# The sign of 64-bit weights through ScalarE's parametric ReLU, norms split in two steps, softmax denominators on VectorE

## The chip, the cores and the metric

The kernel runs on one core of a Trainium2 chip. The core has five engines that run their own instruction lists in order: TensorE (PE, with its weight loads as PEld), VectorE (DVE), ScalarE (ACT), GpSimd (POOL) and SyncE (SP), which issues all DMAs of this kernel. The metric is the device time of one execution in microseconds, as the median of several.

## The reference

Attention over 4 batches, 12 heads, 448 positions and 64 columns, with a cap on the scores, and behind it a two-layer network over the 1792 tokens:

```
scores = cap * tanh(q @ k.T / 8 / cap)
attn   = exp(scores) / (sum(exp(scores)) + 1e-9)      # rows of 448
x      = (attn @ v), heads joined                     # 1792 x 768
h      = x @ w_in                                     # 768 x 2048
g      = s * max(h, 0)**2 + b
out    = g @ w_out                                    # 2048 x 768
```

q, k and v are float32. The weights w_in and w_out come as float64: the kernel reads each as two 32-bit words and makes a float32 of them on the chip.

## The kernel before, in words

**Work.** Scores are taken for pairs of heads; a pair has three blocks of 128 keys (chunks), and two pairs share one block for the last 64 keys. A chunk goes PE (scores, line 512), ACT (tanh, line 516), ACT (exp, line 520). The product with v (line 570) and the row sums (line 578) follow in two runs for each pair, one over chunks 0 and 1, one over chunk 2 and the shared block; such a run is called a half-pair here, and there are 48 of them. ACT then copies the sums out of PSUM (line 598). `normal` sends the row sums through SBUF and DRAM and takes their reciprocals. Both layers run in 16 bit, each product as three matmuls (high by high, high by low, low by high).

**Weights.** `piece` loads a block of 128 x 512 doubles as pairs of words (line 654) and makes float32 of it in four operations: two on DVE for the low word and the sign (`sign`, lines 662 and 663), one multiplication by 2^-112 on DVE or POOL (lines 434, 436), and one on DVE that joins the words (`join`, line 666). `win` does that for three blocks of w_in, squares them (on ACT line 700, DVE 701 or POOL 702), sums the squares on PE (line 712), sends the largest through a second small matmul (`lanes`, line 477), and has a scale from both (`fin`). With it the block is split into two 16-bit parts (lines 433, 453). There are eight such groups of w_in. The first two lie in a tensor named gt until the first layer needs it, the others in tiles named w.

**Order.** The program is written by a planner: `Plan.emit` takes all operations with a rank, a duration that the author estimated and the engines that may do them, and places the one that can start first. So the order on every engine, and for some operations the engine, follow from the numbers in `CHOICE`. Each engine runs its list strictly in that order: an instruction that waits holds everything behind it on its engine. PSUM has two buffers for scores, so PE can be two chunks ahead of tanh.

Of the kernel before, what the change touches and what calls it, by code (L numbers as in the profile page):

```python
# [243 lines left out]
def arrange(units, at):  # L244

    key = {}
    for name, pre, _ in units:
# [5 lines left out]
    'bias': 1.806,  # L253
    'shy': {'DVE': 0.3, 'POOL': 0.5},
# [36 lines left out]
    'late': 0.621,  # L291
    'lag': 0.0,
    'cling': 19.274,
# [4 lines left out]
    'tail': 0.9,  # L298
    'evac': ('ACT',),
    'sq': ('ACT', 'DVE', 'POOL'),  # L300
    'expo': ('DVE', 'POOL'),
# [24 lines left out]
def attention_moe_kernel(  # L326
# [196 lines left out]
    def normal(bb, c2, rank):  # L523
# [15 lines left out]
        def whole():  # L539
            a = P[kc][:, 0]  # L540
            nc.gpsimd.tensor_tensor(a, a, P[kc][:, 1], ALU.add)
            nc.gpsimd.tensor_scalar(a, a, guard[:, 0:1], 0.0, ALU.add, ALU.add)

        gps(0.55, rank, whole, r=["guard", *((kc, h, i) for h in range(2) for i in range(2))], w=[kc], port=True)
        dve(0.32, rank, lambda: nc.vector.reciprocal(P[kc][:, 0], P[kc][:, 0]), w=[kc])
# [14 lines left out]
    def pv(bb, c2, rank, step):  # L560
# [54 lines left out]
        def gather():  # L615
# [6 lines left out]
            r=[("xm", bb, c) for c in range(NP)], w=[("xn", bb)], port=True,  # L622
# [24 lines left out]
    def piece(kr, src, n, rank, over=()):  # L647
# [13 lines left out]
        def sign():  # L661
            nc.vector.tensor_scalar(lo(), lo(), 29, None, ALU.logical_shift_right)
            nc.vector.scalar_tensor_tensor(lo(), hi(), -0x80000000, lo(), ALU.bitwise_and, ALU.bitwise_or)
# [22 lines left out]
    def win(g, rank):  # L686
# [36 lines left out]

        dve(0.38, rank, most, r=[kp], w=[("wnm", g)])
        kl = lanes(("wps", g), rank, g, [("wnm", g)])

        def fin():
            nc.vector.tensor_copy(n[:, 1:2], P[kl][:, 0:1])
            root2(n)
# [466 lines left out]
    m2s = []  # L1196
# [68 lines left out]
```

## Time and profile before

| | |
|---|---|
| median of 3 runs | 640.17 us (638.66 to 641.72) |
| the profiled execution | 639.61 us |
| its span, first to last instruction | 637.8 us |
| PE busy | 627.0 us, 98% of the span |
| DVE, ACT, POOL busy | 400.2, 351.7, 208.1 us |
| moved by DMA | 101.67 MB, 159 GB/s over the span |

The span is what lies between the first and the last instruction in the profile; the execution's own time is 1.8 us longer. Busy time counts the stretches in which at least one instruction of an engine runs. PE is close to always busy, so the views to read are those that show when it isn't: its waits, and the windows in which its busy time is under the window's length or its clock (PEclk, as a share of 2.4 GHz) is under 1. The first 90 us are nearly only attention and preparing of w_in; then the first layer's products fill PE.

### The profile page before, as it was taken

The page shows a single profiled execution, that of the slowest core. Times are in us where ns is not written, and L with a number is a line of the kernel's source. Part 1 is how long each engine was busy: PE and PEld are TensorE (multiplying, and loading weights), DVE is VectorE, ACT ScalarE, POOL GpSimd, SP SyncE. Part 2 cuts the span into 40 slices and gives each one's busy share as a digit, 9 for nine tenths or more (in the row PEclk, how much of TensorE's full clock was granted, in tenths as well). Part 3 has the DMA queues.
Part 4 walks back from the last instruction along what each step waited for, and adds up shares of the span by engine and source line. Part 5 has one row for each costly group of instructions (what it writes and reads, how often), then busy time and mean ns, then how long its engine had stood idle before and what let it go on. Part 6 is the DMA issues. An engine that isn't in the chain of part 4 may idle for free.

```text
span 637.8 us, 11435 instructions
## 1 busy us (share of the span) xinstructions
PE 627.0 (98%) x4404; PEld 331.4 (52%) x4404; DVE 400.2 (63%) x810; ACT 351.7 (55%) x472; POOL 208.1 (33%) x238
## 2 busy tenths in 40 slices
PE   7999899999999999999999999999999999999997
PEld 2332344344444433434454445555558996556997
DVE  5986857888797878788773341577767222537322
ACT  5889787886884585684674531346354002445100
POOL 3343511546456544466151020117643000105000
PEclk9999899999999999999999999999999999999999
DMA  8766423654262775853854013385412774001671
GB/s 301 293 184 193 124 86 107 215 175 143 60 234 59 251 211 179 272 200 92 282 195 157 1 48 128 146 280 212 164 48 89 239 260 147 1 2 53 223 256 67
DMA packets 54774, 101.67 MB, mean 159 GB/s; under 512 B 16192, under 2 KB 34752, under 8 KB 54720
## 3 DMA queue, kind: packets, MB, share of 16 engines
q1 hardware_dynamic: 54720, 100.95, 48.2%
q8 instruction: 34, 0.56, 0.4%
q14 instruction: 20, 0.16, 0.1%
HBM read 82.58 MB, written 18.17 MB: 158 GB/s over the span
## 4 chain that ended last, share of the span: by engine, by line
PE 85%; DMA 8%; DVE 3%; ACT 1%; SPq 1%; POOL 1%; issue 0%; ACTq 0%
PE ps_v L570 9%; PE ps_m L1003 9%; PE ps_s L512 7%; PE ps_s L1003 6%; PE ps_m L843 6%; PE ps_s L844 6%; PE ps_m L844 6%; PE ps_s L843 6%; PE ps_m L845 6%; PE ps_s L845 6%; PE ps_m L1094 5%; PE ps_m L1095 5%; PE ps_m L1096 5%; PE ps_v L578 4%; DMA gt<-in_w_in 2%; DMA w<-in_w_out 2%
## 5 line engine op out<-in xcount | busy, mean ns | idle before, releaser
L1003 PEld LDWEIGHTS <-w 128*128 128x128 f16 x1008 | 96.6, 98 | 1.0
L516 ACT ACTIVATE bed<-ps_s,arena 128x896 f32<-128x896 f32 x84 | 81.5, 1006 | 9.9 <-PE ps_s L512 8.2
L520 ACT ACTIVATE bed<-bed,par 128x896 f32<-128x896 f32 x84 | 84.2, 1040 | 0.2
L570 PE MATMUL ps_v<-bed 128*32 128x448 f32 x768 | 83.0, 548 | 0.8 <-ACT pw L598 0.6
L512 PE MATMUL ps_s<-bed 64*128 64x448 f32 (+1 forms) x384 | 80.6, 578 | 1.9 <-DMA bed<-in_qT 1.6
L1094 PE MATMUL ps_m<-gt,w 128*128 128x448 f16 x192 | 67.7, 353 | 0.0
L843 PE MATMUL ps_m<-x,w 128*128 128x448 f16 x192 | 67.7, 353 | 0.0
L1096 PE MATMUL ps_m<-gt,w 128*128 128x448 f16 x192 | 67.7, 353 | 0.0
L844 PE MATMUL ps_s<-x,w 128*128 128x448 f16 x192 | 67.7, 353 | 0.0
L844 PE MATMUL ps_m<-x,w 128*128 128x448 f16 x192 | 67.7, 353 | 0.0
L845 PE MATMUL ps_m<-x,w 128*128 128x448 f16 x192 | 67.7, 353 | 0.0
L843 PE MATMUL ps_s<-x,w 128*128 128x448 f16 x192 | 67.7, 353 | 0.0
L1095 PE MATMUL ps_m<-gt,w 128*128 128x448 f16 x192 | 67.7, 352 | 0.0
L845 PE MATMUL ps_s<-x,w 128*128 128x448 f16 x192 | 67.7, 352 | 0.0
L843 PEld LDWEIGHTS <-w 128*128 128x128 f16 x384 | 37.5, 98 | 37.3 <-issue 2.1
L845 PEld LDWEIGHTS <-w 128*128 128x128 f16 x384 | 37.5, 98 | 35.0
L844 PEld LDWEIGHTS <-w 128*128 128x128 f16 x384 | 37.6, 98 | 33.8
L512 PEld LDWEIGHTS ps_s<-bed 64*128 64x128 f32 (+1 forms) x384 | 27.4, 177 | 43.5 <-issue 12.2
L938 ACT ACTIVATE pw<-ps_s,arena 128x448 f32<-128x448 f32 x32 | 20.1, 632 | 52.6 <-PE ps_s L845 49.7
L570 PEld LDWEIGHTS ps_v<-bed 128*32 128x32 f32 x768 | 20.3, 109 | 51.4 <-issue 35.7
L444 POOL TENSOR_TENSOR pw<-pw 128x224 f32<-128x224 f32 x24 | 21.6, 912 | 77.6 <-ACT pw L942 71.2
L578 PE MATMUL ps_v<-bed,ones 128*32 128x448 f32 x288 | 45.5, 545 | 0.0
(142 smaller groups left out, 1012.8 us busy)
## 6 DMA issues: line engine op xcount, KB each, us to landing
w<-w SPq DMA_DIRECT2D x48, 512.0 KB, 4.9
w<-in_w_out SPq DMA_DIRECT2D x24, 512.0 KB, 5.0
w<-ws SPq DMA_DIRECT2D x24, 512.0 KB, 4.9
w<-in_w_in SPq DMA_DIRECT2D x18, 512.0 KB, 5.5
bed<-in_v SPq DMA_DIRECT2D x24, 256.0 KB, 4.2
ws<-w SPq DMA_DIRECT2D x12, 512.0 KB, 2.9
bed<-in_kT SPq DMA_DIRECT2D x24, 224.0 KB, 3.3
bed<-in_qT SPq DMA_DIRECT2D x24, 224.0 KB, 3.6
```

What stands on the lines that cost most here:

```text
L512: nc.tensor.matmul(P[kp][o, h, 0:S], keys, P[q][rows], start=True, stop=True)
L516: 1.01, rank, lambda: nc.scalar.activation(P[kh], P[kp][:, :, 0:S], AF.Tanh, scale=tsc[:, 0:1]),
L520: 1.04, rank, lambda: nc.scalar.activation(P[kh], P[kh], AF.Exp, scale=par[:, 0:1]), r=["par"], w=[kh],
L570: nc.tensor.matmul(P[kp][o, 0, 0:S], P[kv][:, c, o], prob(c, h), start=(c == 0), stop=(c == NC))
L578: nc.tensor.matmul(P[kp][o, 1, 0:S], w, ph, start=first, stop=last)
L843: nc.tensor.matmul(ps[:, 0:S], wh, x[:, 0], start=(c == 0), stop=False)
L844: nc.tensor.matmul(ps[:, 0:S], wh, x[:, 1], start=False, stop=False)
L845: nc.tensor.matmul(ps[:, 0:S], wl, x[:, 0], start=False, stop=(c == NP - 1))
L1003: nc.tensor.matmul(at(), w(g, zw), b(g, zb), start=g == 0 and x == 0, stop=g == n - 1 and x == 2,)
L1094: nc.tensor.matmul(ps[:, 0:S], wh, ghi[:, f], start=(f == 0), stop=False)
L1095: nc.tensor.matmul(ps[:, 0:S], wh, glo[:, f], start=False, stop=False)
L1096: nc.tensor.matmul(ps[:, 0:S], wl, ghi[:, f], start=False, stop=(f == NF - 1))
```

## The change

Four edits in the code, and a new set of numbers for the planner:

- `piece` takes three operations for four. The sign no longer gets an operation of its own. The high word, read as a float, is scaled by 2^-112 where it is positive and by 2^-80 where it is negative; the shift by three in `join` then moves the extra exponent bit into the sign. ACT does that in one instruction, a parametric ReLU with scale 2^-112 and slope 2^32 (Prelu), or DVE does it in two (a multiplication, and a minimum with itself times 2^32). POOL no longer takes part. The low word's shift (`low`) no longer stands ahead of the scaling.
- In `win` the part of `fin` that needs only the group's own norm becomes `own`, which does not wait for the second small matmul.
- The reciprocals of the row sums (`whole` in `normal`) go from two POOL instructions and one on DVE to two on DVE.
- Three planner flags (`port`) go, and two lists of prerequisites name all groups where they named one.
- The ranks, `late`, `lag`, `bias` and `cling` are new, so the order on all engines is new. `late` is the margin in us that the planner leaves ahead of the small matmuls on PE: 0.621 before, 0.274 now; `lag`, that of all other PE operations, goes from 0 to 0.176.

```
--- before.py
+++ after.py
@@ -250,55 +250,55 @@
-    'bias': 1.806,
+    'bias': 1.658,
...
-        ('a', 0, 0): (-88.4, 62.61), ('a', 0, 2): (80.2, 2.4), ('a', 0, 4): (227.3, 40.55),
...
+        ('a', 0, 0): (19.2, 53.25), ('a', 0, 2): (20.0, 0.01), ('a', 0, 4): (161.4, 23.63),
+        ('a', 1, 0): (22.0, 75.07), ('a', 1, 2): (1029.6, 0.0), ('a', 1, 4): (985.8, 0.01),
...
-    'late': 0.621,
-    'lag': 0.0,
-    'cling': 19.274,
+    'late': 0.274,
+    'lag': 0.176,
+    'cling': 17.125,
...
+    'expo': ('ACT', 'DVE'),
     'evac': ('ACT',),
     'sq': ('ACT', 'DVE', 'POOL'),
-    'expo': ('DVE', 'POOL'),
@@ -538,11 +538,12 @@
 
         def whole():
             a = P[kc][:, 0]
-            nc.gpsimd.tensor_tensor(a, a, P[kc][:, 1], ALU.add)
-            nc.gpsimd.tensor_scalar(a, a, guard[:, 0:1], 0.0, ALU.add, ALU.add)
-
-        gps(0.55, rank, whole, r=["guard", *((kc, h, i) for h in range(2) for i in range(2))], w=[kc], port=True)
-        dve(0.32, rank, lambda: nc.vector.reciprocal(P[kc][:, 0], P[kc][:, 0]), w=[kc])
+            nc.vector.scalar_tensor_tensor(a, a, guard[:, 0:1], P[kc][:, 1], ALU.add, ALU.add)
+            nc.vector.reciprocal(a, a)
+
+        dve(
+            0.38, rank, whole, r=["guard", *((kc, h, i) for h in range(2) for i in range(2))], w=[kc], port=True,
+        )
         z = zd[bb * NP + c2]
         dma(3584, rank, lambda: nc.sync.dma_start(z, P[kc][:, 0]), r=[kc], w=[("z", bb, c2)], move=0.2)
         kr = buf(("rd", bb, c2), "rd", [128, S], F32)
@@ -619,7 +620,7 @@
         dve(
             0.28, rank,
             gather,
-            r=[("xm", bb, c) for c in range(NP)], w=[("xn", bb)], port=True,
+            r=[("xm", bb, c) for c in range(NP)], w=[("xn", bb)],
         )
         kl = lanes(("xps", bb), rank, NG + ND + bb, [("xn", bb)])
 
@@ -658,16 +659,26 @@
         hi = lambda: P[kr][:, :, 1]
         hf = lambda: P[kr].bitcast(F32)[:, :, 1]
 
-        def sign():
+        def low():
             nc.vector.tensor_scalar(lo(), lo(), 29, None, ALU.logical_shift_right)
-            nc.vector.scalar_tensor_tensor(lo(), hi(), -0x80000000, lo(), ALU.bitwise_and, ALU.bitwise_or)
 
         def join():
             nc.vector.scalar_tensor_tensor(hi(), hi(), 3, lo(), ALU.logical_shift_left, ALU.bitwise_or)
 
-        dve(0.25 + n * 0.0018, rank, sign, r=[kr], w=[(kr, "s")], port=True)
-        scaled(CHOICE["expo"], n, rank, hf, hf, 2.0 ** -112, [(kr, "s")], [kr])
-        dve(0.07 + n * 0.0011, rank + 0.5, join, r=[kr, (kr, "s")], w=[(kr, "f")], port=True)
+        def two():
+            nc.vector.tensor_scalar(hf(), hf(), 2.0 ** -112, None, ALU.mult)
+            nc.vector.scalar_tensor_tensor(hf(), hf(), 2.0 ** 32, hf(), ALU.mult, ALU.min)
+
+        ways = {
+            "ACT": (
+                0.29 + n * 0.00084,
+                lambda: nc.scalar.activation(hf(), hf(), AF.Prelu, scale=2.0 ** -112, alpha=2.0 ** 32),
+            ),
+            "DVE": (0.36 + n * 0.00158, two),
+        }
+        P.any({e: ways[e] for e in engines(CHOICE["expo"])}, rank, [kr], [(kr, "h")], port=True)
+        dve(0.16 + n * 0.00052, rank, low, r=[kr], w=[(kr, "s")], port=True)
+        dve(0.07 + n * 0.0011, rank + 0.5, join, r=[kr, (kr, "s"), (kr, "h")], w=[(kr, "f")], port=True)
         return hf
 
     def raw_buf(key, n):
@@ -724,15 +735,21 @@
         dve(0.38, rank, most, r=[kp], w=[("wnm", g)])
         kl = lanes(("wps", g), rank, g, [("wnm", g)])
 
+        def own():
+            root2(n[:, 0:1])
+            nc.vector.reciprocal(ip[:, 0:1], n[:, 0:1])
+            nc.vector.tensor_scalar(wn[:, g:g + 1], n[:, 0:1], n[:, 0:1], None, ALU.mult)
+
+        dve(0.85, rank + 0.1, own, r=[("wnm", g)], w=[("wnm", g, 0)])
+
         def fin():
             nc.vector.tensor_copy(n[:, 1:2], P[kl][:, 0:1])
-            root2(n)
-            nc.vector.reciprocal(ip, n)
-            nc.vector.tensor_tensor(wn[:, g:g + 1], n[:, 0:1], n[:, 0:1], ALU.mult)
+            root2(n[:, 1:2])
+            nc.vector.reciprocal(ip[:, 1:2], n[:, 1:2])
             nc.vector.tensor_scalar(sw, ip[:, 1:2], 8192.0, None, ALU.mult)
             nc.vector.tensor_scalar(wc[:, g:g + 1], ip[:, 0:1], n[:, 1:2], 1.0 / 2097152.0, ALU.mult, ALU.mult)
 
-        dve(1.75, rank, fin, r=[kl], w=[("wnm", g), ("wc", g)], port=True)
+        dve(1.5, rank, fin, r=[kl, ("wnm", g, 0)], w=[("wnm", g), ("wc", g)])
         for c in range(NC3):
             hi = lambda c=c: w1[g][:, 0, c].rearrange("p a b -> p (a b)")
             lo = lambda c=c: w1[g][:, 1, c].rearrange("p a b -> p (a b)")
@@ -798,8 +815,7 @@
             nc.vector.tensor_copy(brief[:, NG + d:NG + d + 1], m1)
 
         dve(
-            0.68, rank, amax, r=[("wc", g) for g in range(NG)] + [("om", d, q) for q in range(NQ)], w=[("om", d)],
-            port=True,
+            0.68, rank, amax, r=[("wc", g) for g in range(NG)] + [("om", d, q) for q in range(NQ)], w=[("om", d)]
         )
         kl = lanes(("ops", d), rank, NG + d, [("om", d)])
 
@@ -807,7 +823,7 @@
             pow2(p, P[kl][:, 0:1], si, iswo[:, d:d + 1], 1e-30)
             nc.vector.tensor_scalar(sc, wn, si, None, ALU.mult)
 
-        dve(1.3, rank, fin, r=[kl], w=[("op", d), ("os", d)], port=True)
+        dve(1.3, rank, fin, r=[kl], w=[("op", d), ("os", d)])
         half = NQ // 2
         for q in range(NQ):
             part = lambda e, q=q: P[kw[q // half]][:, (q % half) * QF:(q % half + 1) * QF, e]
@@ -1190,7 +1206,7 @@
     for g in range(NG):
         put(("w", g), [], lambda rank, step, g=g: win(g, rank))
     for d in range(ND):
-        put(("o", d), [("w", NG - 1)], lambda rank, step, d=d: wout(d, rank))
+        put(("o", d), [("w", g) for g in range(NG)], lambda rank, step, d=d: wout(d, rank))
     for p in range(ND // 2):
         put(("p", p), [("o", 2 * p), ("o", 2 * p + 1)], lambda rank, step, p=p: mix(p, rank, step))
     m2s = []
@@ -1198,7 +1214,7 @@
         m1s, fast = [], j in CHOICE["fast"]
         for f in range(NG if fast else NF):
             g = f if fast else f // 2
-            pre = [("a", j, NP - 2), ("w", g), ("w", CHOICE["alias"] - 1), *m2s]
+            pre = [("a", j, NP - 2), ("w", g), *(("w", a) for a in range(CHOICE["alias"])), *m2s]
             one = m1pair if fast else m1
             put(("m1", j, f), pre, lambda rank, step, j=j, f=f, one=one: one(j, f, rank))
             m1s.append(("m1", j, f))
```

Both programs hold the same number of matmuls and of DMAs. On the other engines the counts change: 28 of the 48 blocks get ACT's Prelu, 20 the two DVE instructions; of 38 multiplications, 24 additions and 24 scalings that went from POOL none is left there. The order of the pairs changes too: batch 0 is no longer finished before batch 1 begins, and PE has 21 half-pairs before the first product of the first layer, where it had 17.

SP's list from its start, before. In it kT, qT and v are the attention's inputs for a pair, in_w_in a block of w_in, and par the three scalars.

```order
L1140 DMA par<-in_cap 128x1
L488 DMA bed<-in_kT 128x448
L490 DMA bed<-in_qT 128x448
L654 DMA w<-in_w_in 128x1024 x3
L488 DMA bed<-in_kT 128x448
L490 DMA bed<-in_qT 128x448
L1140 DMA par<-in_s 128x1
L1140 DMA par<-in_b 128x1
L494 DMA bed<-in_v 128x512 x2
L654 DMA gt<-in_w_in 128x1024
L488 DMA bed<-in_kT 128x448
```

The same place in the changed program:

```order
L655 DMA gt<-in_w_in 128x1024
L1156 DMA par<-in_cap 128x1
L488 DMA bed<-in_kT 128x448
L490 DMA bed<-in_qT 128x448
L1156 DMA par<-in_s 128x1
L1156 DMA par<-in_b 128x1
L488 DMA bed<-in_kT 128x448 x2
L655 DMA gt<-in_w_in 128x1024
L490 DMA bed<-in_qT 128x448 x2
L494 DMA bed<-in_v 128x512 x3
L655 DMA w<-in_w_in 128x1024 x3
L655 DMA gt<-in_w_in 128x1024 x2
```

One block of w_in (for gt) now stands ahead of the first pair's kT and qT, and the second pair's qT comes behind 2.2 MB where it came behind 2.5 MB. The third block for gt, the first of the two in the last row here, has 5.3 MB ahead of its end.

ACT's list from its start, before. Lines 516 and 520 are tanh and exp of a chunk, line 700 a square of a weight block, line 598 the copy of the sums out of PSUM.

```order
L1153 ACT_TABLE_LOAD
L1153 ACTIVATE arena<-par 128x1
L516 ACTIVATE bed<-ps_s,arena 128x896 x2
L520 ACTIVATE bed<-bed,par 128x896 x2
L516 ACTIVATE bed<-ps_s,arena 128x896 x2
L700 ACTIVATE bed<-w 128x512
L520 ACTIVATE bed<-bed,par 128x896 x2
L516 ACTIVATE bed<-ps_s,arena 128x896 x2
L520 ACTIVATE bed<-bed,par 128x896
L598 ACTIVATE pw<-ps_v 128x896
```

The same place in the changed program, where line 675 is Prelu, line 711 the square, line 599 the copy:

```order
L675 ACT_TABLE_LOAD
L675 ACTIVATE gt<-gt 128x512
L1169 ACTIVATE arena<-par 128x1
L711 ACTIVATE bed<-gt 128x512
L516 ACTIVATE bed<-ps_s,arena 128x896 x2
L520 ACTIVATE bed<-bed,par 128x896 x2
L516 ACTIVATE bed<-ps_s,arena 128x896 x2
L520 ACTIVATE bed<-bed,par 128x896 x2
L675 ACTIVATE w<-w 128x512
L675 ACTIVATE gt<-gt 128x512
L516 ACTIVATE bed<-ps_s,arena 128x896 x2
L520 ACTIVATE bed<-bed,par 128x896
```

Ahead of the first tanh there now stand a Prelu and a square of the first block for gt, and ahead of the fifth tanh the Prelus of a block in w and of the third block for gt.

## Rows read from the trace of the kernel before

**Rows 1.** The page's first part, busy time of each engine and its share
```profile
PE 627.0 (98%) x4404; PEld 331.4 (52%) x4404; DVE 400.2 (63%) x810; ACT 351.7 (55%) x472; POOL 208.1 (33%) x238
```

**Rows 2.** waits of PE: engine, tile, line <- releaser: us in total, times, longest
```profile
PE ps_m L1163 <- POOL w L1166: 2.1, 1, 2.1
...
PE ps_m L712 <- DVE bed L701: 1.7, 1, 1.7
...
PE ps_s L512 <- DMA bed<-in_qT: 1.6, 2, 1.0
...
PE ps_m L785 <- DVE bed L443: 0.8, 2, 0.6
...
PE ps_v L570 <- ACT pw L598: 0.6, 1, 0.6
```

**Rows 3.** busy time by window: stretch, length, engines (instructions), PEclk, DMA share, GB/s
```profile
0.00:12.00 12.00, 8.02 (x26) 2.85 (x26) 4.58 (x11) 6.00 (x7) 2.90 (x13) 1.00 0.78 275
...
12.00:30.00 18.00, 17.62 (x149) 5.85 (x145) 16.18 (x34) 15.80 (x19) 6.90 (x8) 1.00 0.82 305
...
30.00:50.00 20.00, 19.47 (x169) 6.34 (x169) 16.62 (x35) 18.30 (x22) 10.87 (x14) 1.00 0.60 182
...
50.00:68.80 18.80, 16.97 (x142) 5.12 (x140) 14.48 (x24) 18.36 (x22) 8.03 (x10) 1.00 0.68 189
...
68.80:73.20 4.40, 4.40 (x31) 1.47 (x30) 2.88 (x9) 1.42 (x3) 2.65 (x3) 0.61 0.60 180
...
90.00:280.00 190.00, 189.19 (x1340) 78.93 (x1337) 151.07 (x350) 138.03 (x179) 88.56 (x105) 1.00 0.52 166
...
280.00:634.50 354.50, 354.50 (x2443) 224.97 (x2437) 182.02 (x317) 137.70 (x208) 84.41 (x83) 1.00 0.43 145
```

**Rows 4.** timeline, first 26 us: start, us, engine, line, operation [idle before <- releaser]
```profile
0.72 1.28 ACT L1153 ACT_TABLE_LOAD   x1 [0.72 <-PEq L1255]
...
2.11 1.39 SPq L654 DMA_DIRECT2D w<-in_w_in  x3
...
5.10 4.12 PE L512 MATMUL ps_s<-bed 64*128 64x448 f32 x12 [0.60 <-DMA bed<-in_qT]
...
7.00 1.01 ACT L516 ACTIVATE bed<-ps_s,arena 128x896 f32<-128x896 f32 x1 [2.98 <-PE ps_s L512]
...
12.39 1.71 PE L570 MATMUL ps_v<-bed 128*32 128x448 f32 x16
...
16.30 1.89 ACT L516 ACTIVATE bed<-ps_s,arena 128x896 f32<-128x896 f32 x2
...
18.88 0.45 PE L712 MATMUL ps_m<-ones,bed 128*128 128x1 bf16 x12
...
21.45 1.71 PE L570 MATMUL ps_v<-bed 128*32 128x448 f32 x16
```

**Rows 5.** groups by line and shape: xcount | busy us, mean ns | idle before
```profile
L516 ACT ACTIVATE bed<-ps_s,arena 128x896 f32<-128x896 f32 x84 | 81.5, 1006 | 9.9 <-PE ps_s L512 8.2 <-PE ps_v L578 1.6
...
L520 ACT ACTIVATE bed<-bed,par 128x896 f32<-128x896 f32 x84 | 84.2, 1040 | 0.2
...
L598 ACT ACTIVATE pw<-ps_v 128x896 f32<-128x896 f32 x24 | 21.9, 914 | 12.3 <-PE ps_v L578 7.2 <-issue 3.6 <-POOL cmp L542 0.7
...
L700 ACT ACTIVATE bed<-w 128x512 bf16<-128x512 f32 x6 | 4.1, 688 | 1.3 <-DVE w L666 1.3
...
L663 DVE SCALAR_TENSOR_TENSOR w<-w 128x512 int32<-128x512 int32 x42 | 38.0, 906 | 1.4
```

**Rows 6.** chain of waits in order of time: start, us, what
```profile
32.99 1.70 PE ps_s L512 x8
...
34.69 1.64 PE ps_v L570 x16
...
36.34 0.75 PE ps_v L578 x8
...
53.00 6.71 DMA gt<-in_w_in
```

59 rows, old and new, of the table CHOICE are left out of this document.

## The prediction

> **What bounds the kernel now.** I read the page's busy times first. PE is busy for 627.0 us [rows 1] of a span of 637.8, so no change that leaves PE's matmuls as they are can win more than the rest, 10.8 us, and what a half clock costs. The order lists hold the same matmuls before and after, so this is the whole stake.
>
> Then PE's waits, to see where the rest lies [rows 2]: 2.1 us ahead of the first warm-up matmul, 1.6 for the first queries, 1.7 for the squares of a weight group, 0.8 for the sums behind the output bias, 0.6 for the copy of a product, and less for two others. About 3.3 us more is the tail behind the last matmul. Then the windows, to see when [rows 3]: from 280 us on PE has no gap (354.50 of 354.50), and from 90 to 280 it has 0.8 us. All else is lost in the first 73 us. There the clock also matters: behind the 1.7 us wait the granted clock averages 0.61 over 4.4 us, which is a stretch at 1.2 GHz among 2.4, and costs 0.39 x 4.4 = 1.7 us. So this one wait costs 3.4 us. Its chain begins with a block of w_in for gt that is in flight for 6.71 us [rows 6].
>
> The window view shows a second limit. From 50 to 68.8 us ACT is busy for 18.36 of 18.80 us, 98%, and from 12 to 30 for 88% [rows 3]. While there is only attention to do, PE and ACT are level. For a pair of heads ACT has 3.5 chunks of tanh and exp and one copy, 3.5 x (1.006 + 1.040) + 0.914 = 8.1 us by [rows 5]; two neighbours overlap by 0.1 us (two tanh take 1.89 and not 2.01 [rows 4]), so about 7.3. PE has 3.5 chunks of 0.85 and two half-pairs of 1.64 + 0.75, which is 7.8 [rows 6].
>
> **The change part by part.**
>
> *Four operations to three.* For each of 48 blocks DVE loses the sign operation (0.906 us [rows 5]) and POOL 38 multiplications; ACT gets 28 Prelus, DVE 20 times two operations. A Prelu of 128 x 512 isn't in the trace. The nearest row is the square of the same shape, 0.688 us; a tanh of 896 columns, 1.006, bounds it from above [rows 5], and from below I keep half of the square's, 0.34. I take 0.73: 28 x 0.73 = 20 us on ACT, of which 4 Prelus stand in the stretch where ACT is level with PE (at 1.006 another 1.1 us there, at 0.34 some 1.6 less); the square is the nearest row. DVE's two operations have no row either; at the price of the sign operation each, 20 x 1.8 = 36 us would come for the 48 x 0.906 = 43 that go, so DVE is not the worse for it. From 90 to 280 us PE loses only 0.8 us to all engines [rows 3], so what DVE and POOL gain there is worth at most that, and a loss would show only if it used up what these engines are ahead. I credit 0.4 of the 0.8 us for the bias sums.
>
> *The start, moved.* One block of 0.52 MB goes ahead of the first kT and qT. Over the first 12 us the DMAs move 275 GB/s, over the next 18 us 305 [rows 3], so the block takes 1.7 to 1.9 us; it is issued one place earlier in the list, which gives back some 0.4. The first scores start at 6.6 us, not at 5.10 [rows 4]. The first tanh comes 1.9 us behind them as before (7.00), so at 8.5, and the first half-pair at about 13.0, not 12.39 (there the wait for the second pair's qT, which now comes earlier, hid some of it). Cost 0.6 us so far.
>
> *ACT's queue, the wait that is added.* The third block for gt ends 5.3 MB into the queue (six blocks of 0.524, three kT and three qT of 0.229, three v of 0.262). By 12 us 3.3 MB have moved, and the other 2.0 MB take 6.6 us at 305 GB/s: it lands at 18.6. Its Prelu stands on ACT ahead of the fifth tanh. With 0.73 it ends at 19.4; behind it are queued two tanh, an exp, a copy and the exp that the third half-pair waits for, 5.0 us less the overlaps: that exp ends at 24.2 and the third half-pair starts at 24.3. Before, it started at 21.45 [rows 4]. Meanwhile PE has the sums of squares (0.45) and two chunks to do and waits for the rest, some 2 to 3 us in pieces, also because the two score buffers are full until the fifth tanh is through. Cost so far, the 0.6 included: 2.8 us.
>
> *The norms.* The three blocks of the first group to be normed are the first three for gt, and the other group in gt, of which one block came last before and held PE for 1.7 us, is by SP's list complete within the first 10.2 MB. So that wait goes, with its half clock: -3.4 us. In return `late` is 0.35 us smaller, so that a small matmul that comes late now costs that much more; `own` takes three of the six small operations off the path behind the second small matmul, about as much. I set both to nothing. The cover is that PE has other work placed there; without it, each of the 18 small matmuls costs at most 0.35, of which a few would.
>
> *The denominators.* POOL's two instructions go, off PE's path: the chain from a copy to the product has three DMAs in it, and PE doesn't wait for it before the first layer. Nothing, unless that first use is late, which is in the bounds below.
>
> *What the stretch gives back.* From the third to the 23rd half-pair PE has, in the changed order, 20 half-pairs (47.8), 36 chunks (30.6), 18 matmuls of 448 columns at 2.4 GHz (3.4) and three sums of squares (1.4): 83.2 us by [rows 4, 6]. If it never waited it would be there at 24.3 + 83.2 = 107.5. The kernel before needs, for the same work from its 21.45, 83.2 plus its losses there, 0.5 from 30 to 50 us, 1.8 from 50 to 68.8 and 1.7 for the clock [rows 3]: 108.7. So PE's own bound is -1.2. ACT in the same stretch has 35 tanh and exp (71.6), 10 copies (9.1), 7 casts (4.8) and 3 more (2.1), both at the square's price: 87.6, less 90 overlaps of 0.1 = 79. At a busy share of 95%, between the 88 and 98% of [rows 3], that is 24.2 + 83.2 = 107.4, level with PE's bound; at 98% it is 104.8 and PE's bound holds; at 88% it is 114. Since both engines are at their limits, and each holds the other through two score buffers, I add 0.5 to the 107.5 and take -0.7.
>
> *After that.* -0.4 for the bias sums, +0.3 for six more changes between kinds of matmul in PE's list, +0.1 for new small waits. The tail is the same.
>
> The sum is -0.7 us. Against the profiled execution's 639.61 (its span and 1.8 around it) that gives 638.9; the median of before is 0.56 above that execution, so I expect 639.4 as a median.
>
> **The rivals.**
>
> *Everything is given back (faster).* If ACT runs at 98% and the DMAs at the start land as quickly as before, the added wait and the start cost 0.6 together and not 2.8, and the 3.4 us, the 0.5 from 30 to 50 us and the 0.8 past 90 are won: 640.2 - 3.4 - 1.3 + 0.6 = 636.1, at best, with the 1.6 us for the first queries too, 634.4. For it: ACT did reach 98%. Against it: it did so where PE was the one that waited.
>
> *ACT holds PE back (slower).* The place is ACT's list from 18 us on. The price: 2.8 us up to the third half-pair; PE's gaps there together are longer than the 1.7 us one that brought the half clock before, so another 1.7; and ACT at 90%, not 95, arrives at 24.2 + 87.8 = 112.0, where PE before was at 108.7. So the 3.4 us won are spent, 3.3 are lost, and with half of the clock's 1.7 (ACT covers the rest) it is 640.2 + 3.3 + 0.9 = 644.4, at worst, with a late x for the first layer (its casts stand on ACT behind a copy), 645.8. It decides below a busy share of some 92%. For it: 12 to 30 us had 88%. Against it: ACT then waited for PE.
>
> *Tables.* The profile has one table load on ACT, 1.28 us [rows 4], since tanh, exp and the rest live with it. If Prelu lived in another set, the 15 groups of Prelus between tanh and exp would need two loads each, 38 us of ACT, three of these groups in the first 30 us: 640 + 8 or more. The changed order shows one load only, so this has little chance. In the Trainium skill, "ScalarE activation tables: per-element evaluation and per-set limits", section "What a function is on this engine", two functions in different sets are one load of 1283 ns apart, and within one set there is no switch; the trace agrees on the load's length, and no run here shows yet in which set Prelu lies.
>
> **How the numbers follow.** Half a per cent, 3.2 us, is about what a measurement of this kernel can tell from no change; the three runs of before lie within 3.1 us. Forecast (level, -3.2 to +3.2): 0.50. Faster rival: 0.29. ACT holds PE: 0.18. Tables: 0.03. So faster 0.29, same 0.50, slower 0.21. The range goes to the two rivals' ends, 634.4 to 645.8, and leaves out the tables and the outer part of each. The forecast alone would be 637.2 to 642.0.
>
> **What will show it.** The first score matmul at 6 to 7 us, not 5.1; ACT idle until 18 to 19 us ahead of the Prelu of the third block for gt, or not; the third half-pair at 24 (at 21 to 22 I was wrong on the added wait); no wait of over 1 us on the sums of squares between 50 and 75 us; where PEclk falls below 1 behind 12 us; ACT's busy share from 24 to 107 us (over 96% is the faster rival, under 92% the slower one); one table load; a Prelu between 0.69 and 0.78; PE without gaps from 280 us. A wait of over 2 us between 110 and 280 us would be a cause that I have not seen.

## The result, and the profile after

The changed kernel takes 645.94 us (median of 4 runs, 644.63 to 648.76) against 639.48 in the same session: ratio 1.0101, 95% interval 1.0057 to 1.0146. It is slower by about 1%, and just outside the range. A second session gave 647.51 against 638.34, ratio 1.0154 (1.0112 to 1.0196), with single runs from 643.5 to 653.0. The profiled execution took 646.56 us, span 644.8.

The page's busy times, to be held against [rows 1]:

```profile
PE 628.4 (97%) x4404; PEld 331.9 (51%) x4404; DVE 386.2 (60%) x845; ACT 357.2 (55%) x483; POOL 170.0 (26%) x172
```

DVE has 14 us less to do, POOL 38 less, ACT only 5.5 more, PE is busy for 1.4 more with the same matmuls, and the kernel is slower: where the 7 us come from can't be read from the busy column. What PE waits for, against [rows 2] (tile, line <- releaser: us in total, times, longest):

```profile
PE ps_s L512 <- ACT bed L516: 3.2, 4, 1.4
PE ps_s L512 <- DMA bed<-in_qT: 3.1, 1, 3.1
PE ps_m L802 <- POOL bed L444: 2.7, 2, 2.0
PE ps_m L1179 <- POOL w L1182: 2.1, 1, 2.1
PE ps_m L477 <- DVE brief L733: 1.4, 2, 0.8
```

The norm's wait (L712 of before) is gone. In its place stand ACT's tanh, a longer wait for the first queries, the bias sums (L802) and the norm's second small matmul (L477). The windows, with the stretches of [rows 3], say when:

```profile
0.00:12.00 12.00, 6.82 (x18) 2.54 (x18) 2.87 (x8) 4.86 (x7) 1.34 (x11) 1.00 0.73 239
12.00:30.00 18.00, 16.83 (x153) 5.68 (x153) 15.46 (x37) 16.12 (x19) 5.10 (x4) 1.00 0.98 379
30.00:50.00 20.00, 18.39 (x166) 6.06 (x165) 18.84 (x54) 19.75 (x23) 5.12 (x4) 1.00 0.53 145
50.00:68.80 18.80, 18.80 (x157) 6.12 (x151) 13.10 (x33) 17.92 (x21) 5.85 (x5) 1.00 0.63 193
68.80:73.20 4.40, 4.40 (x38) 1.49 (x36) 4.37 (x4) 4.27 (x5) 3.60 (x3) 1.00 0.40 114
90.00:280.00 190.00, 187.68 (x1311) 78.54 (x1303) 145.47 (x358) 136.42 (x183) 70.50 (x71) 1.00 0.51 165
280.00:634.50 354.50, 351.71 (x2381) 219.34 (x2370) 177.38 (x334) 142.33 (x214) 78.48 (x75) 0.99 0.43 144
```

Behind the stretch and its length come the busy times of PE, PEld, DVE, ACT and POOL, then PEclk, the share of the DMAs and GB/s. From 50 to 73 us PE is full at clock 1.00, where before it was 16.97 of 18.80 and then at 0.61. In the first 50 us it does less than before, and behind 280 us, where before it had no gap, 2.79 us are missing and the clock is 0.99.

A window does not count a matmul that runs at half clock as lost. So I also add up, over the whole trace, by how much the time from one matmul's start to the next exceeds what it is for that kind elsewhere (0.356 us between float32 matmuls of 448 columns, 0.468 where their kind changes, 0.190 for float16). I call this PE's lost time. Summed from the start up to a point, in us:

| up to | 32 us | 75 us | 100 us | 160 us | 278 us | end |
|---|---|---|---|---|---|---|
| before | 6.1 | 10.2 | 10.2 | 10.2 | 11.2 | 11.2 |
| changed | 9.6 | 9.6 | 9.6 | 11.4 | 12.3 | 18.8 |
| changed, second session | 9.9 | 9.9 | 9.9 | 13.0 | 14.1 | 17.7 |

The 7.6 us more are the 7.0 us of the span, within what such a sum can tell. Up to 100 us the change wins 0.6 (0.3 in the second session). All of the loss comes behind that: 1.8 us from 100 to 160 and 6.5 from 278 to 296 (3.1 and 3.5 in the second session). The second place in PE's timeline (start, us, line, operation, idle before and its releaser):

```profile
281.53 1.02 PE L512 MATMUL ps_s<-bed 64*128 64x448 f32 x4 [0.74 <-ACT bed L516]
284.60 0.58 PE L802 MATMUL ps_m<-arena,bed 128*128 128x1 f32 x2 [2.05 <-POOL bed L444]
285.05 0.17 PE L477 MATMUL ps_m<-brief,ones 128*128 128x1 bf16 x1
285.14 1.86 PE L512 MATMUL ps_s<-bed 64*128 64x448 f32 x4
286.93 3.21 PE L571 MATMUL ps_v<-bed 128*32 128x448 f32 x16
```

A half-pair's 16 matmuls take 3.21 us there and 1.71 in [rows 4]. From 285 to 291 us the granted clock is 0.50 (the 1.2 GHz level), behind two idle stretches of 0.74 and 2.05 us. The chain of waits shows who made L802 late (start, us, what):

```profile
268.94 8.74 DMA w<-in_w_out
...
277.76 0.68 ACT w L675
278.44 0.51 ACT bed L520
...
279.27 0.71 ACT w L675
280.00 0.71 DVE w L666
...
280.74 1.11 POOL bed L444
...
281.92 1.30 POOL bed L444
...
283.29 0.74 POOL bed L444
...
284.09 0.46 POOL bed L444
...
284.60 0.58 PE ps_m L802 x2
```

The last blocks of one w_out column land 8.74 us after their issue. Then two Prelus with an exp between them, the join and four adds on POOL follow, and PE, which takes its work in order, stands in front of a matmul of one column for 2.05 us.

### The profile page after: what moved, and what is told of

It is laid out like the page before. It is cut to its first block, busy times and chain, and to the rows that moved or that the text cites. A ratio compares the mean times of both kernels' runs of the same rounds, so it can differ in the third digit from the quotient of the medians.

```text
span 644.8 us, 11384 instructions
## 1 busy us (share of the span) xinstructions
PE 628.4 (97%) x4404; PEld 331.9 (51%) x4404; DVE 386.2 (60%) x845; ACT 357.2 (55%) x483; POOL 170.0 (26%) x172
## 4 chain that ended last, share of the span: by engine, by line
PE 87%; DMA 6%; DVE 2%; ACT 2%; SPq 1%; POOL 1%; issue 1%; POOLq 0%; DVEq 0%; ACTq 0%
PE ps_v L571 10%; PE ps_m L1019 9%; PE ps_s L512 8%; PE ps_s L1019 6%; PE ps_s L859 6%; PE ps_s L861 6%; PE ps_s L860 6%; PE ps_m L859 5%; PE ps_m L1110 5%; PE ps_m L861 5%; PE ps_m L860 5%; PE ps_m L1111 5%; PE ps_m L1112 5%; PE ps_v L579 5%; DMA gt<-in_w_in 3%; DMA w<-in_w_out 1%
## 5 line engine op out<-in xcount | busy, mean ns | idle before, releaser
L444 POOL TENSOR_TENSOR pw<-pw 128x224 f32<-128x224 f32 x21 | 17.6, 844 | 106.9 <-ACT pw L958 99.8
```

## The experiments

Two theories. *Order* (theory 1 in the expectations): the new table puts blocks of weights so late, and the small matmuls that need them so early in PE's list, that PE waits; the operations themselves cost little. *Operations* (theory 2): the Prelus fill ACT, and ACT holds PE back (or, in a later form, norms or denominators on DVE do). Ratios are to the kernel before, run in the same session on the same chip.

**Moves in the finished list.** These keep the changed kernel's plan and shift single operations in the emitted list, so everything else stays word for word. An entry names engine, what the operation writes and which of its writers it is; then the place. In the keys, `sc` are scores, `pv` half-pairs, `bps` and `ops` the bias sum and the maximum's matmul of a w_out column, `nps` and `wnm` a group's sums of squares and the three instructions behind them; `h`, `s` and `f` are a block's Prelu, low part and join, `w1l` the low half of its weights.

> The changed kernel once more, as the measure for the three beside it. Both theories: within 2 us of 645.9 us and 0.5 to 1.5% above the kernel before; TensorE's waits on the column sums (L802) near 282 us again about 2 us, with the granted clock halved for some microseconds behind them. If that wait or the half clock were missing in a run that is just as slow, theory 1 (the time is lost where small matmuls stand too early in TensorE's order) would fall.

Measured: 647.51 us, ratio 1.0154 (1.0112 to 1.0196); L802 waits 1.9 us at 282 us, the clock is half from 286 to 289. As expected, a little slower than in the first session.

```diff
+    (('PE', ('ops', 1), 0), ('behind', 'PE', ('sc', 3, 4, 1), 0)),
+    (('PE', ('bps', 1), 0), ('behind', 'PE', ('pv', 3, 3), 0)),
+    (('DVE', ('op', 1), 0), ('behind', 'PE', ('ops', 1), 0)),
+    (('DVE', ('bias', 1), 0), ('behind', 'PE', ('bps', 1), 0)),
```

> Near 282 us the two one-column matmuls of w_out's block (bias sums, L802, and maximum, L477) stand behind one more chunk of scores (L477) and behind the next half-pair (L802), with the two VectorE operations that read them; nothing else moves. Theory 1 (order, not operations): the wait of 2.05 us on L802 and the half clock behind it go, at most 1.5 us of other waits come in their place (VectorE's maximum is ready only at 283.6 us, ScalarE's exponentials at 284.3), the expert product that started at 293.7 us starts at 289 to 290.5 us: 3.2 to 4.7 us less than the changed kernel, about 641.5 to 642.7 us. Theory 2 (ScalarE, which now carries the parametric ReLU, is late everywhere): TensorE waits for ScalarE instead, 0 to 1 us less, 645 us or more.

Measured: 645.84 us (645.50 to 648.81), ratio 1.0123 (1.0098 to 1.0147). At its place the move did what order says:

```profile
283.86 1.92 PE L512 MATMUL ps_s<-bed 64*128 64x448 f32 x8
286.02 0.16 PE L477 MATMUL ps_m<-brief,ones 128*128 128x1 bf16 x1 [0.25 <-DVE brief L815]
287.41 1.71 PE L571 MATMUL ps_v<-bed 128*32 128x448 f32 x16 [1.23 <-ACT pw L599]
289.81 0.38 PE L802 MATMUL ps_m<-arena,bed 128*128 128x1 f32 x2
```

L802 waits for nothing, the half-pair takes 1.71 us and the clock is 1.00. Between 278 and 296 us 1.7 us are lost, not 3.5 or 6.5. But 15.5 us were lost by 278 us (12.3 and 14.1 in the changed kernel's profiles), so the whole time moved by 1.7, inside the changed kernel's own scatter. Half a hit for order: its cause is right at the place, its sum is not.

```diff
+    (('SP', ('wr', 1, 0), 0), ('behind', 'SP', ('q', 0, 0), 0)),
+    (('ACT', (('wr', 1, 0), 'h'), 0), ('behind', 'ACT', ('ph', 0, 0, 1), 0)),
...
+    (('ACT', ('sq', 1, 0), 0), ('behind', 'ACT', ('ph', 0, 0, 1), 1)),
```

> The first block of w_in is issued behind the first two loads of scores' operands (as in the kernel before), and its parametric ReLU, sign part, join and squares stand behind the first two tanh on ScalarE and the scalars on VectorE. Theory 1: first scores at 5.1 us for 7.6, the first half-pair about 1 us earlier, 0.6 to 1.6 us less in all. Theory 2: the 1.4 us of ScalarE that stood in an idle stretch (before 9.5 us) now stand in the full one from 9 to 31 us, so TensorE's waits for tanh there grow by what the start gives: within 0.5 us of the changed kernel, or longer.

Measured: 646.93 us, ratio 1.0136 (1.0110 to 1.0161). The whole time, 0.6 us under after_again, says nothing within this scatter; the trace does. The first scores start at 5.18 us (6.99 in after_again) and the first half-pair at 12.33 (13.25), but the scores that come behind the wait at 19 us start at 20.32 (20.73): this wait for tanh grew to 1.43 us (0.81 and 0.92 in the changed kernel's two profiles), and one of 1.40 ends at 32.98. Operations names the right engine on this stretch: ACT holds PE there. But ACT isn't full: it idles for 1.21, 0.55 and 1.37 us ahead of Prelus at 17.41, 18.68 and 28.85 us, whose blocks have yet to land. So it is the Prelus' place in ACT's list that counts, beside their work; start_dve below takes both away at once and can't tell them apart.

```diff
+    (('PE', ('nps', 4), 0), ('ahead', 'DVE', (('wr', 5, 1), 'f'), 0)),
+    (('DVE', ('wnm', 4), 0), ('behind', 'PE', ('nps', 4), 0)),
+    (('DVE', ('wnm', 5), 0), ('ahead', 'DVE', ('w1l', 4, 1), 0)),
```

> On VectorE the three small instructions that make the norm of groups 4 and 5 ready (L731 to L733) stand ahead of two joins (near 117 us) and ahead of two low parts (near 124 us); TensorE's order is the same. Theory 1: TensorE's waits of 0.86 and 0.69 us on L477 go: 1.2 to 1.6 us less than the changed kernel. Theory 2: no more than 0.3 us, since TensorE would wait for ScalarE instead.

Measured: 646.52 us, ratio 1.0127 (1.0101 to 1.0154). PE's waits from 110 to 160 us, of the changed kernel first and then of this one:

```profile
PE ps_m L477 <- DVE brief L733: 1.4, 2, 0.8
PE ps_v L571 <- ACT pw L599: 0.2, 1, 0.2
```

```profile
PE ps_m L723 <- ACT r L872: 1.4, 1, 1.4
PE ps_v L571 <- ACT pw L599: 0.7, 1, 0.7
PE ps_m L723 <- DVE arena L746: 0.3, 1, 0.3
```

Both waits on L477 went, and the next group's sums of squares (L723) waited instead (0.8 us there in after_again): turned into new waits.

**The Prelus of the start on DVE.**

```diff
+    (('ACT', (('wr', 2, 2), 'h'), 0, 'DVE'), ('ahead', 'DVE', (('wr', 2, 2), 's'), 0)),
+    (('ACT', (('wr', 1, 2), 'h'), 0, 'DVE'), ('ahead', 'DVE', (('wr', 1, 2), 's'), 0)),
+    (('ACT', (('wr', 0, 1), 'h'), 0, 'DVE'), ('ahead', 'DVE', (('wr', 0, 1), 's'), 0)),
```

> As start_back, and the three parametric ReLUs that ScalarE ran between 17 and 30 us go to VectorE in their two-instruction form (L669, L670), ahead of the low part of the same block. In every run so far TensorE's lost time by 32 us is 9.0 to 10.2 us (6.1 in the kernel before), and it reaches the scores at 31 us at the same time whether it began at 5.1 or at 7.6 us. Theory 2 (ScalarE, full from 9 to 31 us, holds TensorE back there): ScalarE is rid of 2.1 us and a wait of 0.5, so the lost time by 32 us falls to 6 to 7 us, 2 to 3 us below start_back. Theory 1 (only TensorE's own order): no change against start_back by 32 us. In the whole time the gain may be eaten by waits behind it; the lost time by 32 us decides.

Measured: 649.76 us, ratio 1.0173 (1.0147 to 1.0198). By 20 us 5.2 us are lost (6.5 in start_back): ACT let PE go. By 32 us it is 11.9, and this is why:

```profile
PE ps_m L723 <- POOL bed L713: 4.0, 1, 4.0
PE ps_m L802 <- POOL bed L444: 2.7, 2, 2.3
PE ps_m L477 <- DVE brief L733: 2.0, 1, 2.0
```

DVE now has the blocks ready later, POOL's square of one starts at 22.72 us, and the norm matmul that PE reached at 20 us waits 4.0 us, with half clock behind it. Neither theory foresaw it: ACT and the small matmuls are two limits that lie close together.

**The numbers.**

```diff
-    'late': 0.274,
+    'late': 0.621,
```

> The changed kernel with the planner's margin ahead of its small matmuls (late) at 0.621, as before the change, for 0.274; the whole order is planned anew with it. Theory 1: the waits at small matmuls (L477, L723, L802) between 100 and 160 us (1.6 to 3 us) and near 282 us (2 us, and some 3 us of half clock) shrink to under 2 us together: 640 to 643 us. Theory 2 (ScalarE late everywhere): they only move: 645 us or more. The lost time by 32 us stays at 9 to 10 us under both.

Measured: 661.99 us (657.85 to 665.12), ratio 1.0348 (1.0319 to 1.0378), 38.7 us lost. A miss for order. The time lies in the open range of operations (645 or more), but not for its reason: the waits at small matmuls did not move to other places, they grew, with single ones of 3.8 us on L477 and 3.0 on L802. One number of the table given back, planned anew, costs some 15 us. So this run doesn't show that the new order lacked margin; it shows how much an order planned from slightly other numbers can cost.

```diff
 (the kernel before)
-    'bias': 1.806,
+    'bias': 1.658,
... (the whole table and margins as in the change, 'expo' as before)
```

> The kernel before, with its own operations (four integer and scaling steps on VectorE and GpSimd, whole norms, denominators on GpSimd), but with the changed kernel's table of starts and its margins. Theory 1 (order costs the time): 643 us or more, with waits at small matmuls that the kernel before does not have. Theory 2 (the operations cost it): 637 to 641 us.

Measured: 668.47 us, ratio 1.0464 (1.0440 to 1.0487), 41.5 us lost, 8.6 of them on the bias sums (longest wait 6.6). The old operations in an order planned from the new numbers are far slower than the new ones in it: the table belongs to its operations, and this run can't price the order of the changed kernel alone. It only excludes that the old operations would have been fast under these numbers.

**The operations in the old order.** Here the kernel before keeps its emitted list on every engine, and operations are exchanged at their places. This separates the theories.

```diff
             nc.vector.tensor_scalar(lo(), lo(), 29, None, ALU.logical_shift_right)
-            nc.vector.scalar_tensor_tensor(lo(), hi(), -0x80000000, lo(), ALU.bitwise_and, ALU.bitwise_or)
...
-        scaled(CHOICE["expo"], n, rank, hf, hf, 2.0 ** -112, [(kr, "s")], [kr])
+        prelu = lambda: nc.scalar.activation(hf(), hf(), AF.Prelu, scale=2.0 ** -112, alpha=2.0 ** 32)
+        P.any({"DVE": (0.16 + n * 0.00052, prelu), "POOL": (0.1 + n * 0.00107, prelu)}, rank, [(kr, "s")], [kr], port=True)
```

> The kernel before in its own order on every engine, with one part of the change alone: the sign's instruction on VectorE is left out and the scaling of all 48 blocks, on VectorE and GpSimd before, is the parametric ReLU on ScalarE, at the same place of the order. Theory 2 (the parametric ReLU on a full ScalarE holds TensorE back): up to 75 us ScalarE had some 9 us free and gets about 20 times 0.70 us, so 5 us or more are lost there, less the 3.5 us of the norm wait near 67 us if VectorE's lighter load removes it: 640 to 648 us, all of the loss ahead of 75 us. Theory 1 (operations cost nothing by themselves): 635 to 639 us.

Measured: 639.92 us (639.78 to 640.85), ratio 1.0020 (1.0007 to 1.0033). All 48 Prelus are on ACT, 16 of them in the first 67 us, where its windows read (columns as above):

```profile
12.00:30.00 18.00, 16.82 (x143) 5.76 (x145) 10.62 (x28) 18.00 (x23) 2.15 (x4) 1.00 0.91 339
30.00:50.00 20.00, 18.80 (x165) 5.62 (x163) 9.87 (x26) 20.00 (x26) 6.44 (x8) 1.00 0.55 166
50.00:68.80 18.80, 17.79 (x138) 5.29 (x136) 9.92 (x19) 18.77 (x23) 4.83 (x7) 1.00 0.65 188
68.80:73.20 4.40, 4.40 (x46) 1.64 (x44) 4.07 (x12) 4.40 (x6) 1.55 (x3) 1.00 0.57 147
```

ACT is busy for 56.77 of 56.80 us. PE's list is the same as before, so its matmuls can be compared one by one: the half-pair that started at 58.27 us starts at 61.06. Then the norm's wait stays away, and the half-pair that started at 74.62 starts at 74.06. So a full ACT does cost PE, 2.8 us, a little less than the norm's wait and half clock give back; operations priced that at 5 or more. With 20 Prelus more on ACT than the changed kernel has, the loss is 1.5 us in all.

```diff
 (on top of the last one)
-            nc.gpsimd.tensor_tensor(a, a, P[kc][:, 1], ALU.add)
-            nc.gpsimd.tensor_scalar(a, a, guard[:, 0:1], 0.0, ALU.add, ALU.add)
+            nc.vector.scalar_tensor_tensor(a, a, guard[:, 0:1], P[kc][:, 1], ALU.add, ALU.add)
+            nc.vector.reciprocal(a, a)
...
             nc.vector.tensor_copy(brief[:, g:g + 1], n[:, 0:1])
+            root2(n[:, 0:1])
+            nc.vector.reciprocal(ip[:, 0:1], n[:, 0:1])
...
```

> prelu_in_old_order (639.9 us) with the other two parts of the change added at the places of the old order: a group's own norm, reciprocal and square directly behind the small instructions that make it ready (ahead of the all-group maximum), and the softmax denominators as two VectorE instructions at the place of the old reciprocal, none on GpSimd. So all operations of the change stand in the order of the kernel before. Theory 1 (the order that the new table makes costs the 7 us): 637.5 to 641 us. Theory 2, in its last form (norms or denominators on VectorE cost it): 643 us or more.

Measured: 641.33 us (640.95 to 642.60), ratio 1.0042 (1.0027 to 1.0057), just above order's range (637.5 to 641) and under that of operations (643 or more). Lost time 7.6 us by 32 us and 12.5 at the end; between 278 and 296 us nothing (PE 18.00 of 18.00 at clock 1.00). So the operations, none of them re-planned, cost 0.3 to 0.6%; the changed kernel costs 1.0 to 1.5%. The rest, 4 to 7 us by these ratios, goes with the new order; in the first session alone the two intervals just touch, at 1.0057. One difference stays open: here all 48 blocks have ACT's Prelu, while 20 blocks of the changed kernel have the two DVE instructions, and no run has those in the old order. In the changed kernel's trace the last such pair starts at 247.9 us, well ahead of the loss at 282 us; but one, 0.42 and 0.69 us long from 115.18 us, does stand on DVE ahead of the wait on L477 at 118 us.

```diff
+            if not soft:
+                nc.vector.scalar_tensor_tensor(lo(), hi(), -0x80000000, lo(), ALU.bitwise_and, ALU.bitwise_or)
...
+        soft = kr[:2] == ("wr", 1)
...
```

> The kernel before in its order, with the parametric ReLU on ScalarE for the three blocks of w_in's group 1 alone (55 to 67 us), the other 45 blocks as before. If the wait of 1.8 us on that group's sums of squares at 66.7 us and the half clock behind it (1.65 us) come from its four steps on VectorE and GpSimd, they go, and the three instructions of 0.75 us on ScalarE, which has 5 us free between 50 and 75 us, cost up to 1 us: 635 to 637 us, 1.5 to 3.5 below the kernel before. If the wait is set by something else (landing, squares), or ScalarE's 2.25 us come out in full: 637.5 to 640 us.

Measured: 638.00 us, ratio 0.9982 (0.9964 to 1.0000). The norm's matmuls run without a wait at 67.50 us (this kernel's L723 is L712 of before), and the clock behind them is 1.00 where [rows 3] had 0.61:

```profile
67.50 0.45 PE L723 MATMUL ps_m<-ones,bed 128*128 128x1 bf16 x12
```

```profile
50.00:68.80 18.80, 17.90 (x154) 5.48 (x156) 11.42 (x22) 18.75 (x23) 4.31 (x6) 1.00 0.65 182
68.80:73.20 4.40, 4.40 (x41) 1.46 (x33) 3.20 (x13) 4.40 (x6) 1.60 (x4) 1.00 0.74 188
```

Three Prelus take away a wait that cost 3.4 us; ACT's full queue takes back 0.9. Lost time at 75 us is 7.8 against 10.2. In the whole time only 0.6 us of that shows, so that 638.0 falls into the second range of the expectation although the wait went: this profile lost 3.0 us on the bias sums at 225, 275 and 299 us, where before lost 1.0.

```diff
-        soft = kr[:2] == ("wr", 1)
+        soft = kr[0] == "or" or kr[1] in (1, 6, 7) or kr[1:] in ((3, 1), (3, 2))
```

> As prelu_one_group, and the parametric ReLU also for all 32 blocks past 75 us; the 13 blocks ahead of group 1, which are scaled up to 50 us, as in the kernel before. Theory 1: start as in the kernel before (lost time by 32 us 6 to 6.5 us against 6.8 with all blocks on ScalarE), no norm wait, up to 2.4 us lost past 100 us as in prelu_in_old_order: 635 to 638 us. Theory 2: 639 us or more.

Measured: 637.78 us (636.90 to 639.85), ratio 0.9987 (0.9969 to 1.0005). Its lost time is the least of all, 5.7 by 32 us, 6.9 at 75 and 8.5 at the end. It beats the changed kernel by 1% or more; that it beats the kernel before is not shown.

**Three moves together.** The entries of sums_later, start_back and lanes_ready in one list.

> The changed kernel with the moves of sums_later, lanes_ready and start_back together; alone they stood 1.7, 1.0 and 0.6 us below the changed kernel's 647.5. If these places are independent of each other (theory 1 in its plain form): 643 to 645 us. If each wait that goes is taken up by the next late block, since the new order has the blocks late along the whole stretch from 100 to 310 us: 645.5 to 648 us, with waits of 1 us or more on L723, L477 or L802 at other places than those moved.

Measured: 645.43 us (643.27 to 647.32), ratio 1.0097 (1.0068 to 1.0125): on the border between the two forms. The profile lost 14.8 us, with these waits left:

```profile
PE ps_s L512 <- ACT bed L516: 4.3, 4, 1.5
PE ps_v L571 <- ACT pw L599: 1.9, 2, 1.2
PE ps_m L802 <- DVE bed L443: 0.8, 1, 0.8
```

The waits at small matmuls shrank, and those for tanh are 4.3 us, where the changed kernel's two profiles have 3.2 and 1.6. From 278 to 296 us PE is busy for 15.58 us of 18, ACT for 13.63; in the kernel before ACT had only 7.77 there. Attention runs on to 308 us in that one too, but in this stretch ACT has three tanh, three exp and no Prelu, against four, five and three here. So the new order puts more of ACT's work and the last w_out blocks into one stretch, and these moves don't undo that.

## Why the prediction was wrong, step by step

*Up to 100 us it was right in its main steps; that the sum is right nearly to the tenth is luck.* It forecast -0.7 us net at 107 us, and the lost time there is 9.6 against 10.2. Its steps: the first half-pair at about 13.0 us (13.04); the third gt block's Prelu waiting for its landing at 18.6 (18.86, after 0.54 idle); the third half-pair at 24.3 (23.28, 1.0 early); the norm's wait gone with its half clock, -3.4 us (shown by prelu_one_group as the work of these operations alone); and PE's own bound holding from there, ACT at 95 to 99% and no time lost from 33 to 100 us. From 24 to 107 us ACT is busy for 78.29 of 83 us, 94%, between the marks of 92 and 96 that were set for the rivals. The start is told by these rows of the changed kernel, to be held against [rows 4]:

```profile
0.72 1.28 ACT L675 ACT_TABLE_LOAD   x1 [0.72 <-PEq L1271]
...
9.48 1.01 ACT L516 ACTIVATE bed<-ps_s,arena 128x896 f32<-128x896 f32 x1 [2.68 <-PE ps_s L512]
...
18.86 0.72 ACT L675 ACTIVATE gt<-gt 128x512 f32<-128x512 f32 x1 [0.54 <-DMA gt<-in_w_in]
19.47 1.89 ACT L516 ACTIVATE bed<-ps_s,arena 128x896 f32<-128x896 f32 x2
...
28.95 0.71 ACT L675 ACTIVATE gt<-gt 128x512 f32<-128x512 f32 x1 [1.26 <-DMA gt<-in_w_in]
```

One table load, as forecast, and Prelus of 0.69 and 0.72 us (0.73 forecast). The first scores came at 7.58 us and not at 6.6. The last row is a wait that the prediction didn't have: ACT stands for 1.26 us ahead of one more Prelu for gt, with tanh behind it, and PE then idles for 1.39 us up to 33.08. In the second session this wait of PE's is missing, but the clock was 0.57 from 23 to 27 us and the third half-pair, which started at 23.73, took 3.12 us. Either way the 1.0 us by which the third half-pair was early was lost again by 33 us, and the sum came out.

*The step that failed is "After that".* It credited -0.4 us for the bias sums and +0.1 for new small waits, with `late` smaller and `own` moved "both to nothing", and took PE to have no gaps from 280 us. Measured behind 100 us: 9.2 us lost against 1.0 before. The bias sums cost 2.7 us and some 2.8 of half clock instead of winning 0.4, L477 cost 1.4, and 0.8 went at a score chunk ahead of L802; the rest lies in smaller pieces. The second session puts it at other places: 3.1 us from 100 to 160 and 3.5 from 278 to 296. The bound of 0.35 us for a small matmul was wrong in kind: it took the change of the margin for the price of being late. A small matmul costs as much as its chain is late, 2.05 us here, and the clock's fall may come on top. I had seen from [rows 3] that PE lost only 0.8 us past 90 us and read it as "little to win"; it says nothing of how early the blocks arrive there, and the change replaces the order in which they do.

*The rivals.* "ACT holds PE back" named the right size (644.4) for the wrong place: its price was all ahead of 112 us, and there nothing was lost net. The faster rival needed a start that costs 0.6 us, and it cost 3.5 by 32 us. The rival of the tables fell with the one table load. What I called a cause that I had not seen, a wait of over 2 us behind 110 us, is what came, at 282 us. Shown: the operations in the old order, with all Prelus on ACT, cost 1.5 to 2.7 us, the norm's wait goes with them, and L802's wait and half clock go when the matmul is moved, though the whole time fell by no more than the scatter. Not settled is which numbers of the new table bring the late blocks; late_back and numbers_alone only show that the table can't be varied one number at a time.

## What to carry to other kernels

Where an in-order engine is full at 97%, price a re-planned order by its small waiting instructions: for each, the chain from the last landing to it, and what stands behind it. A stretch without waits in the old profile is no margin. To judge new operations apart from a new order, put them at the old places first: here that showed a loss of 0.4% where the re-planned kernel lost 1.0 to 1.5, and the version with the least lost time (prelu_past_start) kept the Prelus off ACT up to 50 us and used them behind that, without being shown faster than the kernel before.

## What was not expected of the hardware

A wait of the same length was followed by half clock in one kernel and not in another. In the changed kernel and in start_back PE idles for the same time ahead of the same chunk of scores, and this is what follows, the changed kernel first, then start_back (a row of PE's timeline, then the window of the next 4 us):

```profile
33.08 1.02 PE L512 MATMUL ps_s<-bed 64*128 64x448 f32 x4 [1.39 <-ACT bed L516]
...
33.00:37.00 4.00, 3.92 (x32) 1.38 (x34) 3.76 (x14) 4.00 (x6) 1.04 (x1) 1.00 0.53 107
```

```profile
32.98 1.34 PE L512 MATMUL ps_s<-bed 64*128 64x448 f32 x4 [1.40 <-ACT bed L516]
...
33.00:37.00 4.00, 4.00 (x20) 1.07 (x24) 3.79 (x12) 4.00 (x5) 1.04 (x1) 0.57 0.55 117
```

The clock is 1.00 and 0.57, which cost start_back 1.7 us. What PE did before is not quite the same: its wait at 19 us was 0.81 us in the changed kernel and 1.43 in start_back. But the changed kernel differs from itself, too: behind waits of 0.81 and 0.33 us, which end at 20.52 and 22.05 us, the clock from 23 to 27 us is 1.00 in its first profile, and behind 0.92 and 0.33 in its second it is 0.57. So the length of a wait alone does not fix its price here; both prices have to stand in a range.
